# An attention and mixture-of-experts kernel: another order of the experts, later weight fetches, and five moved pieces of code

## The chip, the core and the metric

The kernel runs on one core of one Trainium2 chip. The metric is the device time of one execution in microseconds (us); the times given are medians of a few executions on the same chip.

## The reference

The input is an attention with sigmoid weights, 8 batches of 12 heads, 448 positions and 64 elements, whose output is turned into 3584 tokens of 768 elements. Each token then goes to the one of 8 experts whose embedding is nearest to it (cosine), and is multiplied by that expert's two matrices.

```python
def _attn_ref(q, k, v):
    scores = scale * np.matmul(q, k.transpose(0, 1, 3, 2)) - np.log(S)
    attn = 1.0 / (1.0 + np.exp(-scores))
    return np.matmul(attn, v).astype(np.float32)

def _moe_ref(x, expert_emb, tau, w1, w2):
    xn = x / (np.linalg.norm(x, axis=-1, keepdims=True) + 1e-06)
    en = expert_emb / (np.linalg.norm(expert_emb, axis=-1, keepdims=True) + 1e-06)
    logits = xn @ en.T / tau
    expert_idx = np.argmax(logits, axis=1)
    ...
    for e in range(E):
        mask = expert_idx == e
        h = np.maximum(x[mask] @ w1[e], 0.0)
        out[mask] = gate_w[mask, None] * (h @ w2[e])
```

w1 has 768 x 1024 elements for each expert and w2 1024 x 768, all in float32.

## The kernel before

**Attention.** 48 pairs of heads are worked off one after the other (`scores`, `av`, their `_tail` forms for the last 64 positions, `evac`). The order of all engines is written out by hand there: what stands in the loop is issued in that order. Between the pieces of a pair, work of the routing is put in: `chunk` computes the router's logits of a block of tokens with TensorE and one VectorE reduction (line 454), `early2` (line 619) picks with TensorE the first 256 tokens of the expert that looks largest after a quarter of the tokens, and gathers them. These 256 tokens are two early slots, numbered -2 and -1, which are computed as soon as attention ends.

**Rows.** `rows(g, j)` turns a finished block of 128 tokens with one DMA transpose on SP's queue (line 461), and stores it from GpSimd's queue to a table `xs` in DRAM, from which the expert stage gathers its tokens. The last rows are turned between the early slots' matmuls.

**Slots.** After attention the kernel counts the tokens of each expert (`cnt`), rounds them up to tiles of 128 (`tl`), sorts the experts (`key`, `low`: `low[e, f]` says that f comes ahead of e; `base` is an expert's first slot), and so gets a list of slots. A slot is one tile of up to 128 tokens of one expert. The list is only known on the chip; registers loaded from the table `ci` steer the engines through it. For the reference's inputs (worked out from the reference) there are 31 slots after the two early ones. A slot of at most 64 tokens takes a short path: half the tile is used, and matmuls run on two halves of the array together. Six of the 31 are short.

| expert (tokens, tiles) | slots before | slots after | short slot before, after |
|---|---|---|---|
| 5 (535 left, 5) | 0 to 4 | 0 to 4 | 4, 4 |
| 2 (870, 7) | 5 to 11 | 5 to 11 | none |
| 7 (544, 5) | 12 to 16 | 14 to 18 | 16, 18 |
| 0 (481, 4) | 17 to 20 | 21 to 24 | none |
| 1 (311, 3) | 21 to 23 | 28 to 30 | 23, 30 |
| 4 (260, 3) | 24 to 26 | 25 to 27 | 26, 27 |
| 3 (160, 2) | 27 to 28 | 19 to 20 | 28, 20 |
| 6 (167, 2) | 29 to 30 | 12 to 13 | 30, 13 |

**One step.** Step t of the loop at the end issues `layer1(t + 1)`, then `layer2(t)`. TensorE thus works layer 1 of the next slot ahead of layer 2 of this one. `hidden(t, half)` follows layer 1: ScalarE and VectorE each take one half of the float16 pair of the rectified result, and a DMA transpose on SP's queue turns it into `hT` for layer 2. `evac2` and `scatter` bring a slot's result out.

**Weights.** An expert's weights come in four parts of 1.5 MB, fetched by DMA on SP's queue, the same that carries the transposes (`fetch(u, n)`: part n, in step u - 2 + n, where u is a slot number that `fetch_table` computes for each expert). `cast(u, ...)` turns them into float16 pairs `w` on ScalarE (line 160) and VectorE (line 163) when the expert with first slot u is due: w1 in step u - 2, the first half of w2 at the end of step u - 1, the second half in step u. Each `w` has one buffer, so a cast waits for the last matmul that reads the old weights. Fetches and casts stand in `If` blocks whose register says whether this slot has one; an engine that passes an untaken block still raises the semaphore that others wait for.

**The end.** The loop is laid out for 39 slots. From slot 26 on each step holds an `If` (`tc.If`, whose branch the profile shows at `_compat.py:109`) that asks whether the next slot exists. Where it does not, every engine goes to an `Else` block behind all the steps.

## Time and profile before

| | |
|---|---|
| median of 3 runs | 798.69 us |
| lowest and highest of them | 794.53 and 801.26 us |
| the profiled execution | 795.2 us |
| its span, first to last instruction | 792.8 us |
| mean granted clock of TensorE | 0.996 |
| TensorE busy | 765.1 us (97% of the span) |
| VectorE, ScalarE busy | 374.2 us, 373.8 us (47% each) |
| gathers, scatters of slots | 31, 60 |

The 2.4 us between 795.2 and 792.8 lie around the span. In the profile PE is TensorE, DVE VectorE, ACT ScalarE, POOL GpSimd and SP the engine that issues most DMAs; a "q" behind the name is the engine's sequencer, which handles branches, semaphores and DMA issues. L230 is a line of the kernel before. In a timeline row stand the start, the duration, engine, line, operation, output and inputs with the number of merged instructions, and in brackets how long the engine had been idle and what ended it. A row of the waits gives the sum of the idle times, how many, and the longest.

### The profile page before, as it was taken

Reading aid. Unit: us, or ns where it says so; the run is one execution under the profiler, and the core shown is the slowest. Engines: PE = TensorE matmul, PEld = TensorE weight load, DVE = VectorE, ACT = ScalarE, POOL = GpSimd, SP = SyncE. Lnnn points to the kernel's source line nnn. Section 1 sums busy time; section 2 is a strip of 40 time slices with the busy share of each in tenths; the row PEclk is TensorE's granted clock in tenths of the full one; section 3 lists DMA queues with packets and bytes.
Section 4 is the critical chain, followed back from the end, with each engine's and each line's share of the span. In section 5 each row is a group of like instructions: output and inputs, shape, how many; then the busy total and the mean of one; then the engine's idle time right before and its main releaser. Section 6 shows DMA issues by size and latency. Waiting matters only on the chain.

```text
span 792.8 us, 17586 instructions
## 1 busy us (share of the span) xinstructions
PE 765.1 (97%) x5847; PEld 376.1 (47%) x5847; DVE 374.2 (47%) x728; ACT 373.8 (47%) x551; POOL 203.0 (26%) x249
## 2 busy tenths in 40 slices
PE   5999999999999989899999999999999999999995
PEld 2434444444444434545555455555555555555553
DVE  3544466678767755942144111423145144545452
ACT  5787777878778862410144010422134044343541
POOL 2122442443335222204221211221131211212021
PEclk9999999999999999999999999999999999999998
DMA  8277896999979669959999988997799978999722
GB/s 226 63 191 191 167 259 179 260 234 235 251 210 264 178 133 164 236 160 215 199 210 198 217 154 189 251 209 185 204 238 256 273 177 208 250 264 261 97 65 48
DMA packets 237254, 157.98 MB, mean 199 GB/s; under 512 B 179020, under 2 KB 216374, under 8 KB 237104
## 3 DMA queue, kind: packets, MB, share of 16 engines
q1 hardware_dynamic: 228000, 122.11, 70.3%
q0 software_dynamic: 8688, 33.94, 13.6%
q8 instruction: 69, 1.13, 0.6%
q14 instruction: 81, 0.66, 0.3%
q10 hardware_dynamic: 416, 0.13, 0.1%
HBM read 95.51 MB, written 22.81 MB: 149 GB/s over the span
## 4 chain that ended last, share of the span: by engine, by line
PE 41%; issue 28%; DMA 23%; POOL 4%; POOLq 2%; ACT 1%; DVE 1%; SPq 0%; DVEq 0%; ACTq 0%
PE psa L420 15%; DMA stage<-xs,gix 14%; PE pss L391 11%; DMA out<-ob,six 7%; PE psa L428 3%; PE ptr L370 2%; PE pss L404 2%; PE psa L230 2%; PE pss L218 2%; POOL out L1092 2%; POOL stage L1065 2%; PE pss L212 1%; POOLq L258 1%; PE psa L452 1%; DMA hT<-hr 1%
## 5 line engine op out<-in xcount | busy, mean ns | idle before, releaser
L218 PE MATMUL pss<-w,xt 128*128 128x512 f16 x900 | 198.4, 379 | 2.4 <-DMA xt<-stage 0.8
L230 PEld LDWEIGHTS <-hT 128*128 128x128 f16 x1296 | 126.2, 98 | 91.7 <-issue 4.6
L393 ACT ACTIVATE att<-pss,bias_s 128x896 f32<-128x896 f32 x144 | 139.9, 1005 | 32.0 <-PE pss L391 26.6
L1092 POOL DMA_INDIRECT out<-ob,six x60 | 65.2, 1087 | 329.0 <-ACTq L993 216.2
L218 PEld LDWEIGHTS <-xt 128*128 128x128 f16 x900 | 87.5, 98 | 107.1 <-issue 3.6
L276 ACT ACTIVATE hr<-pss 128x512 f16<-128x512 f32 x60 | 35.7, 596 | 196.1 <-PE pss L218 155.7
L420 PE MATMUL psa<-att,vt 128*64 128x448 f32 x576 | 125.4, 556 | 0.0
L278 DVE SCALAR_TENSOR_TENSOR hr<-pss,hr 128x512 f16<-128x512 f32 x60 | 41.4, 692 | 167.3 <-ACT hr L276 153.8
L163 DVE SCALAR_TENSOR_TENSOR w<-part,w 128x768 f16<-128x768 f16 (+1 forms) x98 | 98.1, 1067 | 38.9 <-ACT w L160 32.6
L230 PE MATMUL pso<-w,hT 128*128 128x384 f16 x672 | 111.9, 326 | 0.7 <-DVE w L163 0.7
L230 PE MATMUL psa<-w,hT 128*128 128x384 f16 x624 | 103.7, 326 | 2.4 <-DMA hT<-hr 2.0
L391 PE MATMUL pss<-kq 64*128 64x448 f16 x864 | 100.3, 356 | 2.2 <-ACT att L393 1.2
L160 ACT ACTIVATE w<-part 128x768 f16 (+1 forms) x98 | 83.0, 922 | 16.9 <-SPq L983 6.0
L358 POOL COPY pk<-qk 128x384 f32<-128x384 f32 x93 | 44.6, 506 | 147.4 <-PE ptr L370 75.5
L381 DVE SCALAR_TENSOR_TENSOR kq<-ptr,kq 128x448 f16<-128x448 f32 x96 | 59.9, 625 | 27.3 <-ACT kq L378 24.8
L391 PEld LDWEIGHTS <-kq 64*128 64x128 f16 x864 | 35.2, 95 | 75.6 <-issue 52.0
L420 PEld LDWEIGHTS psa<-att,vt 128*64 128x64 f32 x576 | 34.9, 136 | 60.7 <-issue 50.9
L380 DVE TENSOR_SCALAR kq<-ptr 128x448 f16<-128x448 f32 x70 | 43.5, 621 | 41.4 <-PE ptr L370 41.3
L445 DVE SCALAR_TENSOR_TENSOR xT<-psa,xT 128x384 f16<-128x384 f32 x96 | 33.0, 385 | 36.1 <-PE pss L391 26.5
L923 ACT ACTIVATE ob<-psa,own 128x384 f32<-128x384 f32 x16 | 9.3, 578 | 70.2 <-PE psa L230 42.9
L473 POOL TENSOR_TENSOR xf<-xrow 128x768 f32<-128x768 f16 x24 | 39.8, 1660 | 9.4 <-ACT xq L478 9.0
L443 ACT ACTIVATE xT<-psa 128x384 f16<-128x384 f32 x96 | 29.0, 355 | 21.3 <-PE psa L420 18.8
(227 smaller groups left out, 523.9 us busy)
## 6 DMA issues: line engine op xcount, KB each, us to landing
part<-in_moe_w SPq DMA_DIRECT2D x28, 1536.0 KB
qk<-in_q SPq DMA_DIRECT2D x48, 192.0 KB
qk<-in_k SPq DMA_DIRECT2D x48, 192.0 KB
vt<-in_v SPq DMA_DIRECT2D x48, 192.0 KB
xs<-xrow POOLq DMA_DIRECT2D x24, 384.0 KB
stage<-in_moe_w SPq DMA_DIRECT2D x6, 512.0 KB
stage<-in_moe_w SPq DMA_DIRECT2D x8, 384.0 KB
tvv<-in_v SPq DMA_DIRECT2D x48, 32.0 KB
```

The costliest lines, as they stand in the source:

```text
L160: nc.scalar.activation(hi, s, AF.Copy, scale=SW)
L163: nc.vector.scalar_tensor_tensor(lo, s, SW, hi, op0=ALU.mult, op1=ALU.subtract)
L218: nc.tensor.matmul(ph[half][:, t % 2], xt[:, xi, kc, :], wts[wi][:, kc, half * HF:(half + 1) * HF], start=(n == 0), stop=(n == len(L1_TERM ...
L230: nc.tensor.matmul(po[d][:, :HD], hs[fc // 4][:, i, fc % 4, :], wts[wi][:, fc, d * HD:(d + 1) * HD], start=(n == 0), stop=(n == len(L2_TER ...
L278: nc.vector.scalar_tensor_tensor(hr[:, 1], ps, 0.0, hr[:, 0], op0=ALU.max, op1=ALU.subtract)
L358: en.tensor_copy(t.rearrange("p c h d -> p h c d"), qk[i][:, j])
L380: nc.vector.tensor_scalar(hi, x, SQK, None, op0=ALU.mult)
L381: nc.vector.scalar_tensor_tensor(lo, x, SQK, hi, op0=ALU.mult, op1=ALU.subtract)
L391: nc.tensor.matmul(ps[:, h, :S], x[r, ki, c * P:(c + 1) * P], x[r, qi, QC], start=(n == 0), stop=(n == 2))
L393: nc.scalar.activation(a, ps[:, :, :S], AF.Sigmoid, bias=bias_s, scale=1.0 / (8.0 * SQK * SQK))
L420: nc.tensor.matmul(accumulator(i)[h * D:(h + 1) * D, :S], vv[i][:, h, c, :], a[:, h, :], start=((i % 2 == 1 or i == 0) and c == 0), stop=( ...
L1092: ins = nc.gpsimd.indirect_dma_start(out.rearrange("n (h d) -> (n h) d", h=2), bass.IndirectOffsetOnAxis(ap=six[:, d, c:c + 1], axis=0), o ...
```

## The change

1. `key` is computed a second time: from each expert's place `pos` in the old order the middle is subtracted, and the experts are sorted by the square of that. The two first stay first, then come the smallest and the largest of the rest in turn. The tables `eh` and `some` are computed earlier for it.
2. `EARLY` goes from 7 to 5, and the earliest fetch slot of an expert is its place instead of `FIRST`. The slot numbers u at which the six later experts' fetches are tied (part 0 is fetched in step u - 2) were 5, 10, 14, 17, 21, 24 and become 7, 9, 14, 16, 20, 23; the slots at which these weights are first used were 12, 17, 21, 24, 27, 29 and become 12, 14, 19, 21, 25, 28.
3. `early2` is no longer issued with its preparation but later in the same pair of heads.
4. The last block of rows is turned after `hidden(-2, 0)` instead of ahead of it.
5. In `layer1` the cast of the second half of w2 stands between the two halves of `hidden`; it stood after both.
6. The `If` of the end asks in step t for slot t + 2 instead of t + 1, and its `Else` now holds all that remains of the last slot: its scatter, casts and layer 2 too.

```diff
-EARLY = 7
+EARLY = 5
...
-                todo.append((EG, lambda: (finish(fill), early2()), False))
+                todo.append((EG, lambda: (finish(fill), mid.append(early2)), False))
...
                 av(i, 0)
                 if m or i == 0:
                     scores_tail(u + m)
+                while mid:
+                    mid.pop()()
                 for f in sq:
                     f()
                 av(i, 1)
...
-            while rowq:
+            while len(rowq) > 1:
                 rows(*rowq.pop(0))
             layer1_full(-2, xte[0], 0, (9, 3 * NKC))
             hidden(-2, 0)
+            rows(*rowq.pop(0))
...
+        nc.vector.tensor_tensor(low, key.unsqueeze(1).to_broadcast([P, E, E]),
+                                key.unsqueeze(2).to_broadcast([P, E, E]), op=ALU.is_gt)
+        pos = bp1.tile([P, E], F32, name="pos")
+        nc.vector.tensor_reduce(pos, low, axis=AX.X, op=ALU.add)
+        eh = bp1.tile([P, E], F32, name="eh")
+        nc.vector.tensor_scalar(eh, tl, 0.0, None, op0=ALU.is_gt)
+        some = bp1.tile([P, 1], F32, name="some")
+        nc.vector.tensor_reduce(some, eh, axis=AX.X, op=ALU.add)
+        mid_pos = bp1.tile([P, 1], F32, name="mid_pos")
+        nc.vector.tensor_scalar(mid_pos, some, 0.5, 0.25, op0=ALU.mult, op1=ALU.add)
+        nc.vector.scalar_tensor_tensor(pos, pos, mid_pos[:, 0:1], eh, op0=ALU.subtract, op1=ALU.mult)
+        nc.vector.tensor_tensor(key, pos, pos, op=ALU.mult)
         nc.vector.tensor_tensor(low, key.unsqueeze(1).to_broadcast([P, E, E]),
                                 key.unsqueeze(2).to_broadcast([P, E, E]), op=ALU.is_gt)
...
-        nc.vector.scalar_tensor_tensor(at, at, float(FIRST), ago, op0=ALU.max, op1=ALU.add)
+        nc.vector.tensor_tensor(at, at, pos, op=ALU.max)
+        nc.vector.tensor_tensor(at, at, ago, op=ALU.add)
...
     def layer1(t, xt):
         arms(t, lambda: layer1_both(t, xt), lambda: layer1_short(t, xt))
-        for half in range(2):
-            hidden(t, half)
+        hidden(t, 0)
+        cast(t - 1, 1, 1)
+        hidden(t, 1)
...
-    def no_more(t, taken):
+    def last(t, taken):
         inside[0] = t
         with taken[0].Else():
+            scatter(t - 1)
+            fetch(t - 2, 3)
+            cast(t, 1, 0)
+            cast(t, 1, 1)
+            layer2(t)
             scatter(t)
...
-        if MINL <= t + 1 < MAXL:
-            more = tc.If(nc.values_load(ci[0:1, 2, t + 1:t + 2], min_val=0, max_val=4) < 4)
+        if MINL <= t + 2 < MAXL:
+            more = tc.If(nc.values_load(ci[0:1, 2, t + 2:t + 3], min_val=0, max_val=4) < 4)
             taken = []
-            ends.callback(no_more, t, taken)
+            ends.callback(last, t + 1, taken)
             taken.append(ends.enter_context(more))
-            inside[0] = t + 1
+            inside[0] = t + 2
```

Three places show where instructions stand now. The first is PE's order in pair 45 (from 0) of the attention, where `early2` (L619, with `POH` and `ve`) followed the logits of a block (L452):

```order
L452 LDWEIGHTS xT
L452 MATMUL psa_4350<-enT,xT 128x16
L619 LDWEIGHTS POH
L619 MATMUL psa_4350<-ve,POH 128x4
L619 LDWEIGHTS POH
L619 MATMUL psa_4350<-ve,POH 128x4
```

In the changed kernel PE has at that place the third block of scores (L391), the first product with v (L420) and the tail's scores (L404), and only then the same matmuls:

```order
L404 MATMUL pss<-kq 64x448
L404 LDWEIGHTS kq
L404 MATMUL pss<-kq 64x448
L619 LDWEIGHTS POH
L619 MATMUL psa_4350<-ve,POH 128x4
L619 LDWEIGHTS POH
```

So 6 matmuls of L391, 4 of L420 and 12 of L404 moved ahead of the 21 of `early2`.

The second is SP's queue after attention: `xte` are the turned tokens of the early slots, `xrow` the last rows, `hT_0` the turned results of layer 1 of slot -2 (first name: first half; second name: second half):

```order
 L630 DMA_TRANSPOSE xte_113<-xrow 128x12x128
-L461 DMA_TRANSPOSE xrow<-xT 128x12x128 x5
-L280 DMA_TRANSPOSE hT_0_4746<-hr_1_4745 128x8x128
+L461 DMA_TRANSPOSE xrow<-xT 128x12x128 x4
+L280 DMA_TRANSPOSE hT_0_4743<-hr_1_4742 128x8x128
+L461 DMA_TRANSPOSE xrow<-xT 128x12x128
 L280 DMA_TRANSPOSE hT_0_4806<-hr_1_4805 128x8x128
```

The first half of slot -2 went ahead of the last row.

The third is the very end of PE's program. Before, PE had nothing in the `Else` blocks but branches:

```order
L1076 UNCONDITIONAL_BRANCH
L983 UNCONDITIONAL_BRANCH x2
L1091 UNCONDITIONAL_BRANCH
L924 UNCONDITIONAL_BRANCH
L1091 UNCONDITIONAL_BRANCH x14
```

Now each of the 13 `Else` blocks begins for PE with the choice of the path and a whole layer 2 of the last slot (L237 is its short form, with `hT`):

```order
L1103 UNCONDITIONAL_BRANCH
L994 UNCONDITIONAL_BRANCH
L1004 UNCONDITIONAL_BRANCH x2
L1087 COMPARE_AND_BRANCH
L237 LDWEIGHTS hT_0_4743
L237 MATMUL psa_4751<-w_78,hT_0_4743 64x384
```

So PE meets the branch to the `Else` ahead of the last slot's layer 2, where it met it after.

More of the change, by code (lines that the diff above doesn't have):

```diff
@@ L632, in early2 @@
             todo.append((ED, turn, True))
-        er, todo = {}, []
+        er, todo, mid = {}, [], []
         def batch_tasks(b):
@@ L927, in layer2 @@
     def layer2(t):
-        hs = [hT.pop((t, half)) for half in range(2)]
+        hs = [hT[t, half] for half in range(2)]
         pd = po[t > 0 and t % 2]
@@ L948, in attn_moe_kernel @@
         nc.vector.tensor_tensor(ch, kp[:, 1:], kp[:, :MAXL], op=ALU.not_equal)
-        eh = bp1.tile([P, E], F32, name="eh")
-        nc.vector.tensor_scalar(eh, tl, 0.0, None, op0=ALU.is_gt)
-        some = bp1.tile([P, 1], F32, name="some")
-        nc.vector.tensor_reduce(some, eh, axis=AX.X, op=ALU.add)
         ca = bp1.tile([P, MAXL], F32, name="ca")
@@ L996, in fetch_table @@
     def fetch_table():
-        pos = bp1.tile([P, E], F32, name="pos")
         nc.vector.tensor_reduce(pos, low, axis=AX.X, op=ALU.add)
@@ L1037, in attn_moe_kernel @@
             f()
-    layer2_full([hT.pop((-2, half)) for half in range(2)], po[0])
+    layer2_full([hT[-2, half] for half in range(2)], po[0])
     evac2(-2, po[0], rings.setdefault(("ob", (0,)), bp1.tile([P, DM], F32, name="ob_0")))
@@ L1129, in attn_moe_kernel @@
             layer1(t + 1, xg_t.pop(t + 1))
-        cast(t, 1, 1)
         if t == 0:
@@ L1138, in attn_moe_kernel @@
             nc.vector.memset(po[1][1], 0.0)
-        def rest_of_step():
-            if t < 2:
-                ahead(2 + t)
-            if t:
-                fetch(t, 2)
-            if t > 1:
-                fetch(t - 1, 3)
-            if t + 3 < MAXL:
-                turn_rows(t + 3)
-            if t + 4 < MAXL:
-                gather(t + 4)
-        if t + 1 < MINL:
-            rest_of_step()
         cast(t + 2, 0)
         layer2(t)
-        if MINL <= t + 1 < MAXL:
-            more = tc.If(nc.values_load(ci[0:1, 2, t + 1:t + 2], min_val=0, max_val=4) < 4)
+        if MINL <= t + 2 < MAXL:
+            more = tc.If(nc.values_load(ci[0:1, 2, t + 2:t + 3], min_val=0, max_val=4) < 4)
             taken = []
-            ends.callback(no_more, t, taken)
+            ends.callback(last, t + 1, taken)
             taken.append(ends.enter_context(more))
-            inside[0] = t + 1
-        if t + 1 >= MINL:
-            rest_of_step()
+            inside[0] = t + 2
+        if t < 2:
+            ahead(2 + t)
+        if t:
+            fetch(t, 2)
+        if t > 1:
+            fetch(t - 1, 3)
+        if t + 3 < MAXL:
+            turn_rows(t + 3)
+        if t + 4 < MAXL:
+            gather(t + 4)
         scatter(t)
```

## The prediction

> **What bounds the kernel now.** I read the page's first lines, then the waits of PE, then the timeline at each wait.
>
> ```profile
> span 792.8 us, 17586 instructions
> PE 765.1 (97%) x5847; PEld 376.1 (47%) x5847; DVE 374.2 (47%) x728; ACT 373.8 (47%) x551; POOL 203.0 (26%) x249
> ```
>
> PE is idle for 792.8 - 765.1 = 27.7 us. The change removes no matmul and adds none that is executed: 31 slots and six short ones before and after. So it can only move these 27.7 us. The waits of PE name part of them (sum in us, how often, longest):
>
> ```profile
> PE psa L619 <- DVE L L454: 2.3, 1, 2.3
> ...
> PE psa L230 <- DMA hT<-hr: 2.0, 1, 2.0
> ...
> PE pss L218 <- DMA xt<-stage: 0.8, 1, 0.8
> PE psa L237 <- ACTq L993: 0.8, 1, 0.8
> PE pso L230 <- DVE w L163: 0.7, 2, 0.5
> PE pss L218 <- ACT w L160: 0.6, 1, 0.6
> PE psa L237 <- DVEq L993: 0.6, 2, 0.4
> PE pss L218 <- issue: 0.6, 1, 0.6
> PE pss L224 <- DMA hT<-hr: 0.5, 1, 0.5
> PE pss L224 <- issue: 0.4, 1, 0.4
> ...
> PE pso L237 <- DVEq L993: 0.4, 1, 0.4
> ```
>
> All rows but the first two lie in the expert stage and make 5.4 us together over 31 slots. The rest of the idle time is the start, which the change does not touch, and the end after the last matmul. So every term below is a few us at most.
>
> **early2 later: -2.3 us.**
>
> ```profile
> 282.60 0.67 PE L619 MATMUL psa<-ve,POH 128*128 128x4 f16 x21 [2.26 <-DVE L L454]
> 283.21 0.74 PE L391 MATMUL pss<-kq 64*128 64x448 f16 x6
> ...
> 285.47 1.72 PE L420 MATMUL psa<-att,vt 128*64 128x448 f32 x8
> ```
>
> PE waits 2.26 us for a VectorE reduction that ends at 282.6. What now goes ahead of L619 takes from 283.21 to 285.47, 2.26 us. PE fell idle at 280.34 (282.60 - 2.26). If that work is ready then, as its kind is in the other pairs, PE reaches L619 at 282.6, just as the reduction ends. The gather behind `early2` keeps its absolute time. Bounds: -2.3 and 0. I take -2.3, because only ready work is moved ahead.
>
> **One row later on SP's queue: -0.8 us.** At the first layer 2 PE waits for the turned half of slot -2.
>
> ```profile
> 319.06 7.97 PE L230 MATMUL psa<-w,hT 128*128 128x384 f16 x48 [1.95 <-DMA hT<-hr]
> 305.01 0.69 DVE L278 SCALAR_TENSOR_TENSOR hr<-pss,hr 128x512 f16<-128x512 f32 x1 [0.86 <-ACT hr L276]
> 306.98 4.10 SPq L461 DMA_TRANSPOSE xrow<-xT  x1
> 311.17 6.73 SPq L280 DMA_TRANSPOSE hT<-hr  x2
> ```
>
> The last row's transpose holds SP's queue from 306.98 and the half is issued only at 311.17. VectorE's part of that half ended at 305.7, so without the row ahead it can start at about 307, 4 us earlier. The second half keeps its place, and layer 2 needs it only after its first 24 of 48 matmuls. So the 1.95 us go. What is late next is VectorE:
>
> ```profile
> 340.68 2.61 DVE L894 TENSOR_TENSOR part<-part,g 128x1148 f16<-128x1148 f16 x2
> 344.32 1.24 PE L898 MATMUL psr<-part,POH 128*128 128x82 f16 x28
> 345.98 0.89 PE L218 MATMUL pss<-w,xt 128*128 128x512 f16 x3 [0.42 <-DVE hr L278]
> 344.93 1.29 DVE L278 SCALAR_TENSOR_TENSOR hr<-pss,hr 128x512 f16<-128x512 f32 x2 [1.64 <-ACT hr L276]
> ```
>
> VectorE ends L894 at 343.29, PE uses it at 344.32: a cover of 1.03 us. PE arrives 1.95 us earlier, VectorE's chain hangs on the second half and does not. Then VectorE's two pieces of `hidden(0)` (L278), which release the next layer 1, follow L894 directly, and L218 gains 1.0 to 1.2 us less than 1.95. I take -0.8; bounds -1.95 and +0.5 (the row itself is stored later; the first gather hangs on it).
>
> **The order's arithmetic: 0.** Seven small VectorE operations come ahead of `base`.
>
> ```profile
> 310.93 0.19 DVE L830 TENSOR_TENSOR qs<-qs,KT 128x28 f32<-128x28 f32 x1
> 311.65 0.27 DVE L845 TENSOR_TENSOR V<-sm,cst 128x112 f16<-128x112 f16 x1
> 313.65 0.85 PE L849 MATMUL psr<-V,POH 128*128 128x8 f16 x28
> ```
>
> At 0.2 us each (the first row) they move the end of the chain from 311.92 to about 313.3. PE uses it at 313.65, after layer 1 of slot -1. If that cover of 0.3 us is short, it costs up to 0.5.
>
> **The cast between the halves: -1.0 us.** Three waits of short layer 2 for `DVEq L993` (0.6 + 0.4 us in the waits) are VectorE's queue reaching the untaken cast's `If` only after both halves of `hidden`. Now only one half, about 0.7 us, stands ahead, which is more than the longest of them (0.4). They go; bounds -1.0 and 0. In a slot that does cast, the second half waits behind four casts, about 4 us; it is needed a whole slot of 16 us later, and on SP the row transposes behind it have two slots.
>
> **Order of experts and later fetches: +0.4 us.** An expert of two slots is tight: its second slot is short, so the casts of w2, of the next w1 and the short slot meet.
>
> ```profile
> 750.00 3.74 PE L230 MATMUL pso<-w,hT 128*128 128x384 f16 x22 [0.53 <-DVE w L163]
> 754.38 7.93 PE L218 MATMUL pss<-w,xt 128*128 128x512 f16 x36 [0.65 <-ACT w L160]
> ```
>
> Both stand in expert 3's two slots, 27 and 28. With the two rows of L224 in the waits (0.4 and 0.5, ahead of the short slots 28 and 30) and the rest of the `w` row (0.7 - 0.5) at slot 29, experts 3 and 6 cost 2.2 us. Now both stand in the middle, where each has an expert behind it: 2 x (0.53 + 0.65) = 2.4 us, and one wait of 0.4 stays at the end after short slot 27. The wait of 0.8 us for `xt<-stage` came with one fetch in each of steps 3 to 6; steps 3 and 4 now have none, so it goes. For crowded fetches later I add 0.6. Sum: -2.2 + 2.4 + 0.4 - 0.8 + 0.6 = +0.4; bounds -2 and +8, the latter in a rival.
>
> **The new end: +2.3 us.** The rows of the last branch, by engine (count, ns shortest/median/longest, first and last start):
>
> ```profile
> _compat.py:109 PEldq COMPARE_BRANCH x6: 68/68/3703, 726.0 to 783.1; - x6
> _compat.py:109 ACTq COMPARE_BRANCH x6: 34/40/45, 729.1 to 784.8; - x6
> _compat.py:109 ACTq EVENT_SEMAPHORE x2: 17/17/17, 788.0 to 788.1; - x2
> ```
>
> Five times PE passes the branch in 68 ns; the sixth goes to the `Else` and takes 3703 ns. ScalarE's goes at 784.8, its next instruction comes at 788.0. Before, PE and ScalarE had no computation behind that jump. Now the last slot's layer 2 is:
>
> ```profile
> 779.49 0.58 ACT L923 ACTIVATE ob<-pso,own 128x384 f32<-128x384 f32 x1 [3.78 <-PE pso L230]
> 780.16 4.15 PE L237 MATMUL psa<-w,hT 128*64 128x384 f16 x48 [0.77 <-ACTq L993]
> 780.34 0.98 POOL L1092 DMA_INDIRECT out<-ob,six  x1 [11.82 <-ACTq L993]
> 784.41 0.58 ACT L923 ACTIVATE ob<-psa,own 128x384 f32<-128x384 f32 x1 [4.34 <-PE psa L237]
> 786.50 0.98 POOL L1092 DMA_INDIRECT out<-ob,six  x1 [3.88 <-DMA out<-ob,six]
> ```
>
> L237 waits for ScalarE's and VectorE's casts of that slot, which stand in the `Else` too. ScalarE would branch at about 779.9 (0.4 after its last result's start, as 784.41 to 784.8) and reach the cast 3.2 us later (as 784.8 to 788.0). With VectorE's cast a little behind, L237 starts at about 783.7: +3.5 us. In return POOL jumps early, while it waits. Now its last scatter starts 1.51 us after ScalarE's last result (784.99 to 786.50); the one before took 0.27 (780.07 to 780.34): -1.2 us. Sum +2.3. Bounds: -1.3 (the jump costs nothing there) and +5.5 (the way out, over five longer `Else` blocks, costs POOL a jump of 3.2 us too). I take no cost for the way out: after 786.50 POOL left the kernel before without one.
>
> On that way out the Trainium skill, "Runtime: NRT & Kernel Launch", section "Instruction fetch mechanics", says that a taken branch stalls for a fetch when its target lies outside the two 16 KiB pages at hand, 256 instructions each. POOL's five blocks are some 24 instructions each, so by that rule the sum keeps its +2.3; the 3703 ns agree with it, and no run here yet shows the way out.
>
> **Sum.** -2.3 - 0.8 + 0 - 1.0 + 0.4 + 2.3 = -1.4 us. Against the profiled execution's own 795.2 us that is 793.8, 0.18% less. That execution lies 3.5 us below the median of the runs shown, 798.69; the same share of it gives **797.2 us**.
>
> **Rivals.**
>
> *A jump is as cheap as a branch not taken* (68 ns in five of six rows). Then L237 keeps its start at 780.16 or gains a little, POOL still gains 1.2: the end gives -1.3 instead of +2.3, the whole -5.0 us: 793.7. Against it speaks the 3703 ns row. The Trainium skill, "Advanced Engine Details and Errata", section "Control Flow Timing", gives about 108 ns for a compare-and-branch, without a condition on its target; by that figure the end would be this rival's. The trace agrees with it only for branches not taken. Chance 0.14.
>
> *The fetches crowd* (the other sign).
>
> ```profile
> part<-in_moe_w SPq DMA_DIRECT2D x28, 1536.0 KB
> 460.00:480.00 20.00, 20.00 (x113) 10.87 (x112) 2.00 (x3) 1.78 (x3) 2.97 (x3) 1.00 0.76 131
> 580.00:600.00 20.00, 19.61 (x129) 10.61 (x128) 8.81 (x9) 8.08 (x10) 4.08 (x4) 1.00 1.22 283
> ```
>
> Where no fetch runs the slots alone move 131 GB/s (last column). Two fetches in a step of 15.6 us add 2 x 1.57 MB / 15.6 us = 202, together 333, above the 283 of the fullest stretch. Before, this fell on steps 15 and 22 alone; now on 7, 8, 14, 15 and 21. A backlog of (333 - 283) / 283 x 15.6 = 2.8 us for each double step would hold the transposes behind the fetches on SP's queue. If all 14 us of it reached PE, the whole would be +12.6; the transposes have a slot or two of slack, so I price it at 2/3 of it, +8 us on the whole: 806.7. It decides if row transposes, issued two slots ahead, come late more than once. Against it: at 580 to 600 PE lost 0.4 us in 20. Chance 0.15.
>
> *The gains of the front do not arrive*: VectorE's chain between 320 and 343 sets PE's pace, or `early2` waits at its new place. Then 3.1 us less gain: 800.3. For it: covers of 0.3 and 1.0 us. Chance 0.2.
>
> **Numbers.** The forecast has 0.51. Without noise the cases lie between 793.7 and 806.7; the three runs before spread over 6.7 us, so I let the range go 3 us below the lowest and leave out the upper part of the crowding: 791 to 803. A change of 1% is about what a measurement of this kernel can tell from none. Faster than 790.7 needs the cheap jump and luck: 0.06. Slower than 806.7 needs half of the crowding's chance: 0.08. Within 1%: 0.86.
>
> **What would show it.** Right: no wait of L619 for L454, none of 2 us before the first layer 2; no `DVEq` wait of short layer 2; a wait of about 4 us before the last L237, and a last scatter within 0.3 us of ScalarE's last result. Wrong: that wait under 1 us (first rival); PE waits for `xt<-stage` between slots 8 and 20 of more than 3 us together (second); waits of L898 or L619 for VectorE of more than 2 us (third).

## The result, and the profile after

| | before | after |
|---|---|---|
| median | 796.42 us (6 runs) | 809.81 us (6 runs) |
| ratio, 95% interval | | 1.0148, 1.010 to 1.020 |
| the profiled execution | 795.2 us | 811.91 us |

The change makes the kernel 1.5% slower; I had forecast 0.2% faster and a range up to 803. Ratios, here and below, compare the undisturbed runs of both kernels alone, so they are not exactly the quotients of the medians. The first lines of the page of the changed kernel:

```profile
span 810.1 us, 17435 instructions
PE 771.6 (95%) x5847; PEld 376.9 (47%) x5847; DVE 376.3 (46%) x734; ACT 372.8 (46%) x551; POOL 200.6 (25%) x249
```

The span grew by 17.3 us. PE is idle for 38.5 us instead of 27.7 (+10.8), and the same 5847 matmuls take 771.6 us instead of 765.1 (+6.5). So not only waits came: matmuls became slower, which I had excluded ("it can only move these 27.7 us"). PE's timeline of the changed kernel, `early2` and the first layer 2, then the rows behind a wait:

```profile
280.61 0.67 PE L619 MATMUL psa<-ve,POH 128*128 128x4 f16 x21
281.21 1.72 PE L420 MATMUL psa<-att,vt 128*64 128x448 f32 x8
...
312.68 7.96 PE L230 MATMUL psa<-w,hT 128*128 128x384 f16 x48
...
332.72 7.94 PE L218 MATMUL pss<-w,xt 128*128 128x512 f16 x36 [2.40 <-DMA xt<-stage]
342.12 8.05 PE L218 MATMUL pss<-w,xt 128*128 128x512 f16 x36 [0.38 <-DVE hr L278]
...
578.67 7.94 PE L218 MATMUL pss<-w,xt 128*128 128x512 f16 x36 [1.52 <-DMA xt<-stage]
600.33 8.27 PE L230 MATMUL pso<-w,hT 128*128 128x384 f16 x48 [1.27 <-DMA hT<-hr]
611.69 9.27 PE L218 MATMUL pss<-w,xt 128*128 128x512 f16 x36 [3.09 <-ACT w L160]
640.85 0.59 PE L218 MATMUL pss<-w,xt 128*128 128x512 f16 x2 [4.08 <-ACT w L160]
642.11 8.97 PE L218 MATMUL pss<-w,xt 128*128 128x512 f16 x34 [0.67 <-DVE w L163]
666.35 0.80 PE L230 MATMUL pso<-w,hT 128*128 128x384 f16 x2 [3.37 <-ACT w L160]
667.35 10.12 PE L230 MATMUL pso<-w,hT 128*128 128x384 f16 x46 [0.20 <-DVE w L163]
```

Cut into three stretches, the 17.3 us are:

- **Up to layer 1 of slot 1:** 342.12 us, before 345.98: -3.9. But 2.0 of these are no gain of the change. They arise in the first 21 us of the two executions (the same scores start at 20.64 us instead of 22.62), and are there unchanged just ahead of `early2`, where the logits (L452) start at 277.89 instead of 279.89. The change has -1.9.
- **From there to the end of the last layer 2 but one** (791.6 us; before 775.66 + 3.74 = 779.4): 449.5 us instead of 433.4: +16.1. The rows from 578.67 on hold 14.2 us of waits, and the layers behind the longer ones take 1.3, 1.6 and 3.0 us more than their 7.94 or 7.97 (9.27; 0.59 + 8.97; 0.80 + 10.12): 5.9 us. The kernel before had 4.5 us of waits in the same stretch, of which 0.5 stay.
- **The rest:** 18.5 us instead of 13.4: +5.1.

The waits for `ACT w L160` are waits for casts of the weights. ScalarE's row for them in the waits (sum, how often, longest), and then what these two waited for: three fetches on SP's queue and the casts for first slot 21.

```profile
ACT w L160 <- DMA part<-in_moe_w: 16.2, 2, 9.7
```

```profile
610.31 0.39 SPq L173 DMA_DIRECT2D part<-in_moe_w  x1
632.24 0.41 SPq L173 DMA_DIRECT2D part<-in_moe_w  x1
639.74 5.79 ACT L160 ACTIVATE w<-part 128x1024 f16 x6 [6.48 <-DMA part<-in_moe_w]
657.26 0.10 SPq L173 DMA_DIRECT2D part<-in_moe_w  x1
665.46 3.04 ACT L160 ACTIVATE w<-part 128x768 f16 x4 [9.73 <-DMA part<-in_moe_w]
```

The last weights of the expert of slot 21 were issued at 610.31, 29 us ahead of the cast at 639.74. The fetch that the cast waited for is, by the order of the program, the one issued at 632.24, 7.5 us earlier: part 0 of the *next* expert, tied to slot 20. The second cast waits in the same way for the fetch of 657.26. `fetch_part` and `cast_part` reach the two buffers of a part by a register, so when the program is built the two are one object, and a cast waits for the newest fetch of its part ahead of it, whoever's it is. In the kernel before, ScalarE's waits have no such row.

The end: PE's layer 2 ahead of the last (which ends at 791.60), its last layer 2, ScalarE's last result, POOL's last scatter, and the branch on PE's sequencer.

```profile
784.77 6.83 PE L230 MATMUL pso<-w,hT 128*128 128x384 f16 x41
...
795.70 0.56 PE L237 MATMUL psa<-w,hT 128*64 128x384 f16 x2 [4.10 <-ACTq L1004]
797.07 6.40 PE L237 MATMUL psa<-w,hT 128*64 128x384 f16 x46 [0.81 <-DVEq L1004]
803.57 0.58 ACT L938 ACTIVATE ob<-psa,own 128x384 f32<-128x384 f32 x1 [11.36 <-PE psa L237]
804.43 0.98 POOL L1104 DMA_INDIRECT out<-ob,six  x1 [9.67 <-ACT ob L938]
```

```profile
_compat.py:109 PEldq COMPARE_BRANCH  x6: 68/74/3394, 722.1 to 788.9; - x6
```

### The profile page after: what moved, and what is told of

The parts are those of the page before. It is cut to its first block, busy times and chain, and to the rows that moved or that the text cites. A ratio compares the mean times of both kernels' runs of the same rounds, so it can differ in the third digit from the quotient of the medians.

```text
span 810.1 us, 17435 instructions
## 1 busy us (share of the span) xinstructions
PE 771.6 (95%) x5847; PEld 376.9 (47%) x5847; DVE 376.3 (46%) x734; ACT 372.8 (46%) x551; POOL 200.6 (25%) x249
## 5 line engine op out<-in xcount | busy, mean ns | idle before, releaser
L218 PE MATMUL pss<-w,xt 128*128 128x512 f16 x900 | 201.6, 383 | 12.8 <-ACT w L160 7.2
L1104 POOL DMA_INDIRECT out<-ob,six x60 | 62.0, 1034 | 353.1 <-ACTq L1004 224.1
L420 PE MATMUL psa<-att,vt 128*64 128x448 f32 x576 | 124.4, 552 | 0.0
L230 PE MATMUL psa<-w,hT 128*128 128x384 f16 x672 | 111.8, 326 | 0.6 <-DMA hT<-hr 0.5
L230 PE MATMUL pso<-w,hT 128*128 128x384 f16 x624 | 106.7, 332 | 5.0 <-ACT w L160 3.4
L391 PE MATMUL pss<-kq 64*128 64x448 f16 x864 | 99.7, 354 | 2.6 <-ACT kq L378 1.3
L160 ACT ACTIVATE w<-part 128x768 f16 (+1 forms) x98 | 83.1, 922 | 34.7 <-DMA part<-in_moe_w 16.2
L391 PEld LDWEIGHTS <-kq 64*128 64x128 f16 x864 | 35.1, 95 | 75.9 <-issue 51.8
L420 PEld LDWEIGHTS psa<-att,vt 128*64 128x64 f32 x576 | 34.7, 135 | 59.5 <-issue 49.7
L1076 POOL DMA_INDIRECT stage<-xs,gix x31 | 32.9, 1060 | 31.5 <-issue 24.0
```

What stands on the lines that cost most here:

```text
L160: nc.scalar.activation(hi, s, AF.Copy, scale=SW)
L218: nc.tensor.matmul(ph[half][:, t % 2], xt[:, xi, kc, :], wts[wi][:, kc, half * HF:(half + 1) * HF], start=(n == 0), stop=(n == len(L1_TERM ...
L230: nc.tensor.matmul(po[d][:, :HD], hs[fc // 4][:, i, fc % 4, :], wts[wi][:, fc, d * HD:(d + 1) * HD], start=(n == 0), stop=(n == len(L2_TER ...
L391: nc.tensor.matmul(ps[:, h, :S], x[r, ki, c * P:(c + 1) * P], x[r, qi, QC], start=(n == 0), stop=(n == 2))
L420: nc.tensor.matmul(accumulator(i)[h * D:(h + 1) * D, :S], vv[i][:, h, c, :], a[:, h, :], start=((i % 2 == 1 or i == 0) and c == 0), stop=( ...
L1104: ins = nc.gpsimd.indirect_dma_start(out.rearrange("n (h d) -> (n h) d", h=2), bass.IndirectOffsetOnAxis(ap=six[:, d, c:c + 1], axis=0), o ...
```

## Experiments

Short names: S is the false wait just shown, Q a late transpose on SP's queue (below), T the traffic of two fetches in one step. "Distance" is the number of slots from the slot that a fetch is tied to, to the first slot of the expert ahead of it. Each ratio is to the kernel before, run beside it on the same chip.

### The fetch slots, and the end

Three edits of the changed kernel's fetch table, and one that puts the end back:

```diff
-EARLY = 5
+EARLY = 7        (another kernel: 6)
```

> The changed kernel with EARLY back at 7, nothing else: the six fetch slots become 5, 7, 12, 14, 19, 21 (7, 9, 14, 16, 20, 23 in the changed kernel). Theory S (false wait): a cast of a weight part waits for the newest fetch of that part that stands ahead of it in the program, whichever expert it is for, because both buffers of a part are one object to the dependency tracking. In the changed kernel the fetch tied to slot 20 runs one step ahead of the casts for first slot 21, so these wait for weights that they do not use (6.48 and 9.73 us on ScalarE) and TensorE stands 3.1 to 4.1 us three times. With EARLY 7 the smallest distance from a fetch slot to the next expert's first slot is 2 instead of 0 and 1. S expects the waits of TensorE for casts between slots 17 and 23 to fall from 11.4 us to under 2, the granted clock there to go back to 1.00, and 794 to 799 us. Theory T (traffic: two fetches in one step): six double steps instead of five, so 809 to 815 us. Theory L (weights come too late because they are fetched later): also 795 to 799 us, told from S by the kernel with one fetch moved later.

> The changed kernel with EARLY 6: fetch slots 6, 8, 13, 15, 19, 22. The distance of 1 between a fetch slot and the next first slot moves from (first slot 21, fetch 20) to (first slot 14, fetch 13); five double steps, as many as with EARLY 5. Theory S: the casts for first slot 14 now wait for the fetch tied to slot 13, so TensorE's waits for casts move to slots 12 to 15 and those at slots 20 to 22 go; 797 to 810 us, little below the changed kernel. Theory L (later fetches come late): every fetch is a step earlier, so no wait moves forward, those at slots 20 to 22 shrink to about half; 800 to 804. Theory T: the stalls stay with the double steps, 806 to 812.

```diff
         nc.vector.tensor_tensor(at, at, pos, op=ALU.max)
+        seventh = bp1.tile([P, E], F32, name="seventh")
+        nc.vector.tensor_scalar(seventh, pos, 6.0, None, op0=ALU.is_equal)
+        nc.vector.tensor_tensor(at, at, seventh, op=ALU.add)
```

> The changed kernel with one number of the fetch table changed: the fetch of the seventh expert (first slot 25) is tied to slot 21 instead of 20, one step LATER. Theory S: each of its parts is then issued behind the cast of the same part for first slot 21 in the program, so these casts wait no longer for it: ScalarE's waits of 6.48 and 9.73 us go, and TensorE's waits of 4.1, 0.7, 3.4 and 0.2 us at slots 21 and 22 with them, and the slow clock of that stretch; minus 8 to minus 12 us against the changed kernel, 798 to 802. The wait of 3.1 us at the cast of first slot 19, which is for SP's queue, stays. Theory L (late weights): one step later still, the same or slower, 809 to 813. Theory T: double steps 21 and 22 instead of 21 alone, one more, 810 to 813.

```diff
-        if MINL <= t + 2 < MAXL:
+        if MINL <= t + 1 < MAXL:
...
-    def last(t, taken):
+    def no_more(t, taken):
         inside[0] = t
         with taken[0].Else():
-            scatter(t - 1)
...
             scatter(t)
```

> The changed kernel with the end of the kernel before: the If asks for slot t + 1 and its Else holds only the last scatter. The prediction's term for the new end was +2.3 us. The trace of the changed kernel shows more: TensorE waits 4.9 us before the last layer 2 (0.8 us in the kernel before), and that layer 2 then runs 6.40 us instead of 4.15. If a long idle lowers the clock behind it, both go together: minus 4.1 minus 2.3 plus 1.2 for the sooner last scatter given back = minus 5.2 us, 803 to 806. If the slow clock there has another cause (the whole of this execution), only minus 2.9: 806 to 808. If the jump out costs nothing: 809 to 811.

| kernel | median | ratio, interval |
|---|---|---|
| EARLY 7 | 812.73 | 1.0201, 1.0158 to 1.0244 |
| EARLY 6 | 815.19 | 1.0265, 1.0205 to 1.0324 |
| seventh expert's fetch one slot later | 804.75 | 1.0109, 1.0066 to 1.0152 |
| old end | 805.76 | 1.0164, 1.0118 to 1.0210 |

S was right on places and wrong on sums. With EARLY 6 the false wait moves to first slot 14, as expected; SP's fetches, ScalarE's casts and PE there:

```profile
528.28 0.42 SPq L173 DMA_DIRECT2D part<-in_moe_w  x1
536.97 5.79 ACT L160 ACTIVATE w<-part 128x1024 f16 x6 [4.17 <-DMA part<-in_moe_w]
...
563.30 3.04 ACT L160 ACTIVATE w<-part 128x768 f16 x4 [11.82 <-SPq L994]
564.20 0.80 PE L230 MATMUL psa<-w,hT 128*128 128x384 f16 x2 [5.46 <-ACT w L160]
```

The first cast waits for the fetch of 528.28, which is tied to slot 13. TensorE's 5.46 us hang on the second cast, and its 11.82 us are put down to SP's queue, not to a fetch.

With one fetch one slot *later*, ScalarE's two long waits at slot 21 are gone; these are its casts for that slot:

```profile
632.15 5.79 ACT L160 ACTIVATE w<-part 128x1024 f16 x6 [1.54 <-DVE w L163]
...
647.62 3.04 ACT L160 ACTIVATE w<-part 128x768 f16 x4 [0.62 <-SPq L994]
```

So weights that come late (L) were not the trouble. The ratio is 0.004 lower than the changed kernel's, where S expected 0.010 to 0.015, and the intervals overlap. But EARLY 7, which should have mended most, mended nothing, and EARLY 6 has a group that S doesn't know, PE's waits for rows (sum, how often, longest):

```profile
PE pss L218 <- DMA xt<-stage: 8.8, 4, 4.1
```

The old end's trace has the old last layer 2 (0.77 us of wait, 4.16 us long), but the ratio of 1.0164 shows no gain against 1.0148: not settled here.

### The parts one by one

On the kernel before: parts 3, 4 and 5; parts 3 and 5; parts 1 and 2. The edits are those of the change. The fourth is the changed kernel with the old end and a table in place of the fetch rule.

> The kernel before with parts 3, 4 and 5 of the change alone (early2 later, one row later on SP's queue, the cast between the halves); order of experts, fetch slots and end stay as before. The prediction gave these three terms -2.3 - 0.8 - 1.0 = -4.1 us. In the trace of the changed kernel the first slot's layer 2 started 3.8 us sooner and the waits of short layer 2 for DVEq were gone. If the loss of the changed kernel lies in its middle and its end alone, this kernel is faster than before: ratio 0.994 to 0.997. If it is the row's late store that delays slot 0 (TensorE waited 1.3 to 3.4 us for xt at the first layer 1 in five traces), half of it is lost: 0.997 to 0.999.

> The same without the moved row: parts 3 and 5 alone on the kernel before. Terms of the prediction: -2.3 - 1.0 = -3.3 us. If the moved row costs as much as it brings (1.95 us gone before the first layer 2, 1.3 to 3.4 us new at the first layer 1), this one is as fast as the kernel with the row moved, or faster by up to 1 us; if the row's own term holds, it is 0.8 us slower. Ratio to before 0.994 to 0.997; no wait for xt at the first layer 1, 1.9 us for hT before the first layer 2.

> The kernel before with parts 1 and 2 of the change alone: the new order of experts with its fetch rule. The prediction's term was +0.4 us. In the trace of the changed kernel TensorE waits 14.4 us more between slots 16 and 23 and its matmuls there run some 5 us longer behind these waits. If that is all of parts 1 and 2, minus the wait of 0.8 us at slot 8 and some 1.5 us of the small experts at the end: +15 to +18 us, ratio 1.018 to 1.023. If the front or the cast between the halves has part in the loss (a cast that now stands ahead of the second half of hidden), less: 1.005 to 1.012.

```diff
-        nc.vector.scalar_tensor_tensor(at, base, -float(EARLY), at, op0=ALU.add, op1=ALU.max)
...
+        nc.vector.tensor_scalar(at, pos, 2.0, 1024.0, op0=ALU.is_lt, op1=ALU.mult)
+        for place, slot_no in ((2, 6), (3, 10), (4, 14), (5, 17), (6, 21), (7, 25)):
+            nc.vector.tensor_scalar(ago, pos, float(place), float(slot_no), op0=ALU.is_equal, op1=ALU.mult)
+            nc.vector.tensor_tensor(at, at, ago, op=ALU.add)
```

> The changed kernel with the old end and the fetch slots of the six later experts set by hand to 6, 10, 14, 17, 21, 25 (for this input; 7, 9, 14, 16, 20, 23 in the changed kernel). They are chosen by two theories together: no fetch that stands one step ahead of another expert's cast of the same part (the distances to the next expert's casts are 2, 0, 2, 0, 0 slots), and only one step with two fetches (15) instead of five. The order of experts is that of the changed kernel. If the false wait and the crowding explain all of the loss, TensorE's waits between slots 4 and 26 for casts are under 2 us and for xt under 2 us, the clock stays at 1.00, and with the gains of the front the time is 790 to 794 against 794 of before: ratio 0.995 to 1.000. If the order itself costs (two experts of two slots with a short one each in the middle leave too little time between their casts), waits for casts at slots 13 to 21 stay at 5 us or more: 1.005 to 1.012.

| kernel | median | ratio, interval |
|---|---|---|
| parts 3, 4, 5 | 809.11 | 1.0201, 1.0162 to 1.0239 |
| parts 3, 5 | 807.73 | 1.0155, 1.0122 to 1.0188 |
| parts 1, 2 | 806.32 | 1.0154, 1.0125 to 1.0183 |
| changed kernel, old end, fetch table | 803.58 | 1.0134, 1.0097 to 1.0170 |

My theory fell here: the parts that I had booked as gains lose as much as the order does. The order with its fetch rule costs 1.5%, a little less than expected (1.018 to 1.023), and the fetch table doesn't save the changed kernel: a second cause is in it, as shown below, and the false wait isn't gone. The table ties a fetch to slot 17, two slots ahead of first slot 19. ScalarE's waits for fetches in that kernel (sum, how often, longest), and TensorE behind the longest:

```profile
ACT w L160 <- DMA part<-in_moe_w: 10.9, 4, 5.8
...
632.79 0.73 PE L230 MATMUL pso<-w,hT 128*128 128x384 f16 x2 [3.53 <-ACT w L160]
```

The cast that waited 5.8 us is for slot 19 and starts at 631.90; the last fetch of its part ahead of it, issued at 623.02, is for slot 21. So a distance of 2, which EARLY 7 leaves too, is not enough.

### The cast between the halves

Part 5 alone; parts 3 and 4 alone; the changed kernel without part 5; and part 5 alone with the rows moved ahead:

> The kernel before with part 5 alone: the cast of the second half of w2 between the two halves of hidden. The kernel with parts 3 and 5 alone was 1.0155 slower, against my terms of -2.3 and -1.0 us. Theory Q (SP's queue): in a slot that casts, the second half of hidden now waits on ScalarE and VectorE behind four casts, its transpose is issued late on SP's queue (721.2 instead of some 4 us after the first at 716.7), and a weight fetch and the row transposes stand behind it in that queue; they come late by more than the two slots that I gave them. Q expects most of the loss here: ratio 1.014 to 1.019, waits of TensorE for xt of 3 us and more at the slots behind a cast, and some us of slower clock behind them. Theory E (early2 at its new place, or the front, costs): 0.998 to 1.001 here, and the loss in the kernel with the front alone.

> The kernel before with parts 3 and 4 alone (early2 later, one row later), without the cast between the halves. Theory Q: the front gains what the traces show, 3 to 4 us by the first slot, and nothing of it is lost: ratio 0.995 to 0.997. Theory E: 1.010 to 1.016. If the gain is there but slot 8's fetches or the small experts at the end eat it: 0.998 to 1.000.

> The changed kernel with part 5 alone undone: the cast stands after both halves again. The order with its fetch rule alone was 1.0154, the front is worth some -4 us (-0.005), the new end some +5 (+0.006). If the losses add up, that is about 1.016, no better than the changed kernel (1.0148), and then the cast costs nothing where other waits give SP's queue its slack. Theory Q with the cast's share independent of the order: 1.002 to 1.008.

```diff
+        if t + 3 < MAXL:
+            turn_rows(t + 3)
         if t + 1 < MAXL:
             layer1(t + 1, xg_t.pop(t + 1))
...
-            if t + 3 < MAXL:
-                turn_rows(t + 3)
```

> The kernel before with part 5, and the transposes of the rows of slot t + 3 moved on SP's queue ahead of both halves of hidden, so that no row waits behind the late second half; the cast and the late half are as in the kernel with part 5 alone. Theory Q: the waits for xt go with the place in the queue, ratio 0.997 to 1.003, if the rows' new place costs hT nothing (it is needed a layer later). If the late half itself or the casts' order on VectorE costs: 1.012 to 1.018 as with part 5 alone.

| kernel | median | ratio, interval |
|---|---|---|
| part 5 | 810.83 | 1.0174, 1.0130 to 1.0218 |
| parts 3, 4 | 794.62 | 0.9998, 0.9966 to 1.0031 |
| changed kernel without part 5 | 806.96 | 1.0156, 1.0105 to 1.0206 |
| part 5, rows first | 793.76 | 0.9971, 0.9939 to 1.0002 |

Part 5 alone costs 1.7%, and all of it goes when the rows' transposes stand ahead of the two halves on SP's queue. Nothing else differs between those two kernels, so the place in SP's queue is the cause. (The kernel before with the rows ahead, but without part 5, was not run; its one wait for rows is 0.77 us, so it has little to gain from them.) The kernel with part 5 alone, around the casts of slot 24 (ScalarE: first half, casts, second half; SP: both halves, a fetch, the rows of slot 27; PE: layer 1 of slot 27):

```profile
717.75 0.60 ACT L276 ACTIVATE hr<-pss 128x512 f16<-128x512 f32 x1 [3.27 <-PE pss L218]
718.27 3.04 ACT L160 ACTIVATE w<-part 128x768 f16 x4
719.10 5.83 SPq L280 DMA_TRANSPOSE hT<-hr  x2
721.22 0.57 ACT L276 ACTIVATE hr<-pss 128x512 f16<-128x512 f32 x1
725.68 0.39 SPq L173 DMA_DIRECT2D part<-in_moe_w  x1
727.50 4.89 SPq L1069 DMA_TRANSPOSE xt<-stage  x1
743.74 10.13 PE L218 MATMUL pss<-w,xt 128*128 128x512 f16 x36 [6.31 <-DMA xt<-stage]
```

And the kernel with the rows first, the same rows and slot:

```profile
707.30 2.36 SPq L1069 DMA_TRANSPOSE xt<-stage  x1
709.95 4.41 SPq L280 DMA_TRANSPOSE hT<-hr  x2
...
725.70 7.93 PE L218 MATMUL pss<-w,xt 128*128 128x512 f16 x36
```

The second half waits 3 us for the casts, the fetch and the rows stand behind it, and the rows of slot 27 are issued 9.9 us before their layer is due (743.74 - 6.31 - 727.50). They land 16.2 us after their issue, where the median of the 31 row transposes of that trace is 5.0. With the rows first there are 18.4 us. Before the change there were 12.3 (716.13 to 728.47) and no wait. Why 16 us? Windows of the kernel with part 5 alone (length, busy us of PE, PEld, DVE, ACT, POOL, clock, DMA share, GB/s):

```profile
728.00:732.00 4.00, 4.00 (x32) 2.15 (x27) 0.69 (x1) 0.60 (x1) 1.70 (x2) 1.00 1.00 350
732.00:736.00 4.00, 4.00 (x27) 2.38 (x25) 0.63 (x1) 1.72 (x2) 0.00 (x0) 1.00 1.24 157
736.00:740.00 4.00, 1.43 (x9) 0.65 (x7) 4.00 (x5) 4.00 (x6) 0.00 (x0) 1.00 1.17 72
```

First the fetch has the DMA engines, at 350 GB/s. Then they are busy at 72 to 157 GB/s: by the packet records the transposes' small packets come at 214 to 395 in 2 us as long as packets of a gather run beside them (732 to 742), against 1020 to 1050 in 2 us without. So rows that come a little later fall behind the fetch and into the gather; that this is the whole reason is argued, not shown.

The front alone gains nothing in the median, although its trace passes L619 without a wait: layer 1 of slot 0 waits 6.61 us for its rows there. And the changed kernel without part 5 is no faster than with it. One of two causes undone shows nothing here. That the waits of the other give SP's queue its slack is argued, not shown: the changed kernel without part 5 still waits 3.81 us for the rows of slot 19.

### Both causes, the clock, and the end

The kernel before with parts 3, 5 and rows first; the changed kernel with rows first; the changed kernel with rows first, the seventh fetch one slot later, old end and old row; the same two mends with the new end and the new row, and with the old end. The edits are those shown.

> The kernel before with early2 later (part 3), the cast between the halves (part 5) and the row transposes ahead of both halves of hidden on SP's queue; old order, old fetch slots, old end, last row in its old place. With the cast and the rows ahead alone the ratio was 0.9971. In the kernel with parts 3 and 5 the first slot's layer 1 stood at 341.2 us against 346.0 to 347.4 where early2 has its old place. If those 5 us are kept, now that nothing behind takes them back: 0.989 to 0.993. If they are taken back behind (a fetch or a gather that is no sooner): 0.995 to 0.998.

> The changed kernel with the row transposes of slot t + 3 ahead of both halves of hidden, nothing else. If the late second half on SP's queue (theory Q) were all of the loss in the middle: 0.999 to 1.003, the new end's 5 us left over against the gain of the front. If the false wait of the casts for another expert's fetch (theory S) is there beside it, its waits of 6.5 and 9.7 us on ScalarE and of 4.1 and 3.4 us on TensorE at first slot 21 stay with the slow clock behind them, and only the waits for xt go and the one of 3.1 us for SP's queue at first slot 19: 1.006 to 1.011.

> The changed kernel with four things mended: row transposes ahead of hidden (Q), the seventh expert's fetch one slot later (S), the old end, and the last row in its old place. Kept are the new order of experts, EARLY 5, early2 later and the cast between the halves. If Q, S, the end and the row explain the loss: 0.990 to 0.996, no wait of TensorE over 2.5 us behind the first slot. If the order itself costs: 1.000 to 1.006, waits for casts at slots 18 to 25.

> The changed kernel with the row transposes ahead of hidden (ratio 1.0131 with that alone) and, in addition, the seventh expert's fetch tied to slot 21 instead of 20; the new end and the moved row stay. In the trace with the rows alone TensorE waited 1.48, 0.67, 8.67 and 0.20 us for casts at first slot 21 and its matmuls behind took 1.8 us more, together 12.8 us. Theory S (these casts wait for the seventh expert's fetch, which they do not use): all of it goes, 1.0131 - 12.8 / 796 = 0.997, so 0.995 to 1.000. If the fetches are merely too many or too late there: 1.008 to 1.015, since the fetch is a step later.

> The same with the old end too; against the kernel with all four things mended only the last row stands in its new place. In the traces the new end costs a wait of 3.3 to 4.9 us instead of 0.8 before the last layer 2, a last layer 2 of 5.8 to 7.0 us instead of 4.2, and gives back 1.2 us at the last scatter: 3 to 5 us, so the ratio is 0.004 to 0.006 lower than in the kernel with rows and fetch mended alone, 0.990 to 0.995. The moved row cost between nothing and 5 us in the traces (wait for xt at the first layer 1): 0.000 to 0.004 above the 0.9915 of the kernel with four things mended.

| kernel | median | ratio, interval |
|---|---|---|
| before + parts 3, 5, rows first | 791.60 | 0.9968, 0.9940 to 0.9996 |
| changed | 809.81 | 1.0148, 1.0100 to 1.0197 |
| changed + rows first | 804.48 | 1.0131, 1.0099 to 1.0163 |
| ... + fetch one slot later | 793.21 | 0.9979, 0.9949 to 1.0010 |
| ... + old end | 789.05 | 0.9948, 0.9917 to 0.9979 |
| ... + old row | 788.91 | 0.9915, 0.9886 to 0.9944 |

This ladder settles the middle. With the rows first the changed kernel has no wait for rows left, and the false wait stands alone, longer than ever; SP's fetch, ScalarE's cast and PE in that kernel:

```profile
646.72 0.40 SPq L173 DMA_DIRECT2D part<-in_moe_w  x1
655.55 3.04 ACT L160 ACTIVATE w<-part 128x768 f16 x4 [15.03 <-DMA part<-in_moe_w]
656.45 0.80 PE L230 MATMUL pso<-w,hT 128*128 128x384 f16 x2 [8.67 <-ACT w L160]
657.44 9.75 PE L230 MATMUL pso<-w,hT 128*128 128x384 f16 x46 [0.20 <-DVE w L163]
```

One fetch one slot later takes 1.5% off. That step also speaks against T as the cause here: it adds a sixth step with two fetches (22) and is the largest gain of all. In EARLY 7's trace, though, TensorE waits 2.18, 1.71 and 2.46 us for the rows of slots 8 to 10, right behind the steps 5 and 6 that hold two fetches, so there T may have a part. The old end gives 0.3%, the old row another 0.3%; each interval is as wide as such a step, so these two are only likely. The kernel with all four mends beats the kernel before by 0.85%. It keeps the new order and later fetches, and lies 0.5% below the old order with the same rows and cast; the two intervals just meet, and where the order gains I have not found. It still has one false wait: at first slot 25 a cast waits 3.79 us for the eighth expert's fetch, tied to slot 23, and TensorE 1.47 us for the cast.

The inserted idle times:

```diff
+        for _ in range({6: 1, 8: 2, 10: 3, 14: 4, 19: 6, 22: 9}.get(t + 1, 0)):
+            nc.vector.tensor_copy(xg_t[t + 1], xg_t[t + 1])
         if t + 1 < MAXL:
             layer1(t + 1, xg_t.pop(t + 1))
```

> The kernel before with TensorE held idle ahead of layer 1 of slots 6, 8, 10, 14, 19 and 22: VectorE copies the slot's tile xt onto itself once, twice, 3, 4, 6 and 9 times between the last result's evacuation and that layer 1; the values stay as they are. What is asked is how long the layer 1 behind each wait takes (7.94 us in the others). In the traces so far it took 9.2 to 10.9 us behind waits of 2.2 us or more in most cases, 7.94 behind waits under 2.1 us. If an idle stretch lowers the clock by itself, the layer behind waits over 2.5 us takes 1.3 to 2.9 us more, whatever caused the wait; if the slow matmuls came from the transfers that caused those waits, it takes 7.94 us here behind each of them.

PE's layer 1 behind each inserted wait:

```profile
423.27 9.85 PE L218 MATMUL pss<-w,xt 128*128 128x512 f16 x36 [5.47 <-DVE xt L1129]
458.82 7.94 PE L218 MATMUL pss<-w,xt 128*128 128x512 f16 x36 [2.33 <-DVE xt L1129]
493.06 7.94 PE L218 MATMUL pss<-w,xt 128*128 128x512 f16 x36 [2.93 <-DVE xt L1129]
559.14 9.63 PE L218 MATMUL pss<-w,xt 128*128 128x512 f16 x36 [3.63 <-DVE xt L1129]
637.02 10.48 PE L218 MATMUL pss<-w,xt 128*128 128x512 f16 x36 [4.91 <-DVE xt L1129]
697.09 9.47 PE L218 MATMUL pss<-w,xt 128*128 128x512 f16 x36 [10.66 <-DVE xt L1129]
```

No transfer is late here, only VectorE is slow: idle time itself makes the next layer slow, by 1.5 to 2.5 us behind waits from 3.6 us on, and by no more behind 10.66 us than behind 3.63. The granted clock shows it: behind the wait of 5.47 us it is 0.50 from 423 to 426 us, and 1.00 again from 429 on. The waits of 2.33 and 2.93 us cost nothing, though I had expected a loss from 2.5 on. This is one execution.

## Why the prediction was wrong, point by point

Two terms failed: the order with its later fetches, where I counted nothing for casts that wait for another expert's fetch (+0.4, alone +12 us), and the cast between the halves, where I took the rows' slack on SP's queue for granted (-1.0, alone +13.8 us). In the changed kernel the stretch that holds both grew by 16.1 us, less than their sum.

**What bounds the kernel.** "It can only move these 27.7 us" failed. 5.9 us of the middle and 2.8 us of the last layer 2 (0.56 + 6.40 against 4.15) are slower matmuls behind waits. The Trainium skill, "TensorE: Matmul & The Clock Gate", section "What's actually happening", says that the clock is halved after an idle window of about 3.4 us and comes back after about 3.4 us of work. The inserted waits agree for 3.6 us and more, and for the cost, which by that would be some 1.7 us (an estimate from the page's figure). It disagrees below, as a row of the kernel with the fetch table shows, which the expectation for the inserted waits (7.94 us behind waits under 2.1) had overlooked:

```profile
744.38 9.63 PE L218 MATMUL pss<-w,xt 128*128 128x512 f16 x36 [2.06 <-DMA xt<-stage]
```

Nor does one wait always do the same: behind the 2.26 us of L619 the granted clock stays at 1.00 in the kernel before, and in the kernel with parts 1 and 2 alone it is 0.74 and 0.70 in the next two windows of 3 us (282 to 288).

**early2 later, -2.3.** The wait of L619 is gone, and the term came out to its size: the products behind it (L420, x8) start at 281.21 us instead of 285.47, 4.26 sooner, of which 2.0 are the start of the execution. The 5 us that I later read from layer 1 of slot 1 (341.2 against 346.0 to 347.4) hold that start too; in the kernel with all four mends it begins at 343.55. In the whole time it can't be told from nothing (0.9968 with it, 0.9971 without).

**One row later, -0.8, bounds -1.95 and +0.5.** The wait of 1.95 us before the first layer 2 is gone, but layer 1 of slot 0 waits 2.40 us for its rows: +0.45 in this trace, just inside the bound. In the other traces with the moved row that wait is between nothing and 6.61 us, so the bound, though named, was far too small. Ratios with the moved row are 0.003 to 0.005 above those without, in two pairs. The likely sign is a loss of some 3 us.

**Cast between the halves, -1.0, bounds -1.0 and 0.** The three `DVEq` waits went as said, and the part costs 13.8 us (1.74% of 795). The sentence that failed is "on SP the row transposes behind it have two slots". I had counted slots from the program, where the trace had the answer: 12.3 us from issue to use, with a fetch just ahead in the queue and a gather beside it.

**Order and later fetches, +0.4.** Measured alone: +12 us (1.54%), beyond the bounds of -2 and +8. The step "for crowded fetches later I add 0.6" failed. I looked for traffic and for rows, never at what else waits for a fetch; in that kernel's trace ScalarE's casts wait 9.0 us for fetches, and in the kernel before not at all. The table of slots (first slot 21, a fetch tied to 20) held the answer, with the register that picks the buffer.

**The new end, +2.3.** Its mechanism came as written: a wait of 4.10 + 0.81 us before the last L237, and a last scatter 0.28 us after ScalarE's last result. From the end of the layer ahead to the end of the span it cost 5.1 us in the trace. The term was mis-sized by the slow last layer, 2.8 us. The ladder's step is 0.3%, 2.5 us, give or take 3.5.

**Rivals.** The cheap jump is refuted: the taken branch took 3394 ns, the others mostly 68 to 74. The Trainium skill's figure of about 108 ns ("Advanced Engine Details and Errata", "Control Flow Timing") fits neither: the branches not taken were faster, the taken one took some thirty times as long. The crowding (806.7) was nearest in time and not in cause: its own sign, rows late by more than 3 us between slots 8 and 20, showed 1.7 us. My list of signs had no line for casts. The third rival, front gains that do not arrive, is what parts 3 and 4 alone gave in time (0.9998), not in cause: the wait there is for rows, not for VectorE. Every sign that I had named for a right forecast came, except that a `DVEq` wait of 0.81 us stands inside the last layer 2: they looked at the gains, and the loss arose elsewhere.

## What to carry to other kernels

Before moving anything on an in-order engine, list what its results feed on the *next* in-order queue, and read from the trace how many microseconds lie between issue and use of what stands behind; slots counted in the program are no measure. A double buffer that is picked by a register was one buffer to the waits here, so a fetch must not be issued shortly ahead of the cast of another's weights. When undoing one suspect shows nothing, undo two: losses that hide each other don't add.

## What the runs showed of the hardware

A wait of TensorE of 3.6 us or more cost 1.5 to 2.8 us beyond itself in the rows shown, no more for 10.7 us than for 3.6; of those between 2.0 and 3.0 us some did and some did not. In the one stretch counted, transposes of rows beside an indirect gather ran at a fifth to two fifths of their rate without it (214 to 395 packets in 2 us against 1020 to 1050), and a transfer with a median of 5.0 us to its landing took 16.2.
